# Half of the output weights' combinations move from the expert stage to the gate/value stage, and packed rows are loaded and turned later

## The chip, the cores and the metric

The kernel runs on one core of a Trainium2 chip. The metric is the time of one execution on the device in microseconds (us), median of three runs. TensorE is called PE here, VectorE DVE, ScalarE ACT, GpSimd POOL and SyncE SP. All engines run their own instruction streams and wait for each other through semaphores. DMAs are issued by SP (loads from the inputs) and by POOL (what is stored to and loaded back from DRAM buffers of the kernel, and the indirect ones).

## The reference

Three parts follow one another, all in float32.

```python
def _attn_ref(q, k, v):                      # 4 batches, 12 heads, 448 rows, 64 columns
    scores = scale * np.matmul(q, k.transpose(0, 1, 3, 2)) - np.log(S)
    attn = 1.0 / (1.0 + np.exp(-scores))
    return np.matmul(attn, v)
...
x = np.ascontiguousarray(attn_out.transpose(0, 2, 1, 3)).reshape(B * S, H * D)   # 1792 x 768
...
for e in range(E):                           # _moe_ref: 8 experts, each token to its best one
    mask = expert_idx == e
    h = np.maximum(x[mask] @ w1[e], 0.0)     # 768 -> 1024
    out[mask] = gate_w[mask, None] * (h @ w2[e])
...
gate = 1.0 / (1.0 + np.exp(-(x @ w_gate)))   # _moe2_ref: 768 -> 1536
val = x @ w_val
return (gate * val @ w_out)                  # 1536 -> 768
```

## The kernel before

**Stages.** Attention runs over 24 head pairs and writes rows to a DRAM buffer `xd`. Routing chooses an expert per token. The expert stage takes 14 token tiles of 128 rows, numbered p, and scatters its results to the DRAM buffer `yd`. The gate/value stage and the output stage then run twice, for two halves of 896 rows (`sb` 0 and 1). Their products are done in the way of Strassen, with seven products for eight, so they need sums and differences of weight blocks and of rows ahead of the products. Every float32 operand is split into a high part (ACT copies it, L271 for the expert weights) and a low part (DVE subtracts, L272), and each product is three matmuls.

**Order in the expert stage.** Loop p runs: four `h_chunk(p, c)` (first weights, L1086), the front of p+1 (gather, transposes), four `y_chunk(p-1, c)` (second weights, L1070 to L1072), `y_out(p-1)`, `turn(p)`. `y_out` scales on ACT (L1132) and scatters the tile into `yd` by an indirect DMA of POOL (L1138). After each chunk `split_next` splits the weight chunk that is four ahead into a ring. `turn` transposes h and makes its two parts (`hh` on ACT, `hl` on DVE at L1111). A few small tiles go another way, with `yq` (L1203) as their scatter; their rows are gathered early, and transposed on PE at p = 3 (`xTq`, L1163). Each program line is put on its engine's stream where the Python code stands, so where a call stands in these loops sets what it waits behind.

**Side work hidden in the loops.**

- *Packed weights.* The last stages' weights come packed in 64 bits (`wffP`). `decode_load` loads 1.5 MB through SP, `decode(k, step)` unpacks in three DVE operations (L234, L237, L240) and stores 768 KB by POOL: gate/value weights to `wd[k]`, output weights to `wob[0]`. Most are decoded in attention, four (`DEC_MOE`) in the expert stage at p = 4 to 7, and five (`DIRECT`) in the gate/value stage from the staging tile `stg` into the room `dec`, from which they are used and also stored for the second half.
- *Combinations of the output weights.* `combine_load(k)` loads one of six parts of `wob[0]` (768 KB, L254) into a room `cb`, `combine(k)` makes four sums on DVE (L259 to L262) and stores to `wob[1]` (L263). All six stand in the expert stage, two per p from `COMBINE` = 8: one in h_chunk, one in y_chunk, after c = 1. The first two loads are issued at the end of p = 7.
- *Packed rows.* `y_load(t)` loads 128 finished rows of `yd` (384 KB, L1283, into one of two slots), `y_turn(t)` transposes them on PE (L1295) and copies to `YB` on ACT (L1299), for t = 0 to 6. `YLOADS` gives which are loaded at the end of which p; they are turned in the next p, after y_chunk c = 1 and c = 3. `y_split` makes parts of the rows (L1340, L1341).

**The last stages.** `gv_group` runs the twelve groups g of the gate/value stage; `hooks(n)` puts side work behind the products of a group at seven places (`at_`). In the last group the rows for the output stage are split (`t_split`, L1560, L1561) and the sums of the first results prepared (`s_prep`, L1598, L1600). p2, p5, p6 and p7 are the last four products of a group; each is followed by DVE adding its result (L1443, L1448, L1449) to `G`.

```python
def decode_load(k, src, dst):
    SP.dma_start(src.bitcast(U32), wffP[k].bitcast(U32))
...
            if c == 1 and 0 <= k6 < NWO:
                combine(k6)
                if k6:
                    combine_load(k6 + 1)
...
        for t in YLOADS.get(p, ()):
            y_load(G, t)
```

Of the kernel before, what the change touches and what calls it, by code (L numbers as in the profile page):

```python
# [17 lines left out]
ALU = mybir.AluOpType  # L18
# [49 lines left out]
DIRECT = [3, 5, 7, 9, 11]  # L68
DECODE_IN = {1: 3, 2: 5, 4: 7, 6: 9, 8: 11}
DEC_ORDER = list(range(KF2, NDEC)) + [k for k in range(KF2) if k not in DIRECT] + DIRECT  # L70
YLOADS = {7: (0, 1), 8: (2, 3), 9: (4, 5), 10: (6,)}
COMBINE = 8


_COLS = {}
# [72 lines left out]
def routed_kernel(ctx: ExitStack, tc: tile.TileContext, kqP, vP, emb, tau, w1P, w2P, wffP, cst, out):  # L148
# [98 lines left out]
    def wo_part(i, k):  # L247
        return wob[i][:, :, k * 384 : (k + 1) * 384]

    def combine_room(k):  # L250
        return buf(f"cb{k % 2}", (SB_XA, k % 2 * CH), CH)

    def combine_load(k):
        G.dma_start(combine_room(k).rearrange("p (a m) -> p a m", m=384), wo_part(0, k))  # L254

    def combine(k):

        x = combine_room(k).rearrange("p (a m) -> p a m", m=384)
        V.tensor_sub(x[:, 3], x[:, 2], x[:, 3])  # L259
        V.tensor_tensor(out=x[:, 0], in0=x[:, 3], in1=x[:, 0], op=ALU.add)  # L260
        V.tensor_sub(x[:, 2], x[:, 2], x[:, 0])
        V.tensor_sub(x[:, 1], x[:, 1], x[:, 0])  # L262
        G.dma_start(wo_part(1, k), x)  # L263


    parts = {}
    done_split = [0]
# [1088 lines left out]

    decoded = buf("dec", (SB_G, FH * SB + 2 * YA), CH)

    def w_raw(sb, g, a, b):
        if sb == 0 and g in DIRECT:  # L1360
            return decoded[:, a * YW : b * YW]
        return w_part(g, a, b)

    def w_his(sb, g, half):
# [64 lines left out]
    def gv_group(sb, g, hooks):  # L1429

        i, val = divmod(g, 2)
        a, b, d = [one_bank[2 * k + g % 2][:, :TH] for k in range(3)]
        s1, u2, u4 = temp(sb, "s"), temp(sb, f"u{val}"), temp(sb, "v")
        sg = [temp(sb, f"g{k}") for k in range(4)]

        def mm(o, w, y, first, last):
            product(o, *w_op(sb, g, w), *yop[y], KH, first, last)

        def out(k, ps, u=None):
            f, th = (i, i, i + FH, i + FH)[k], k % 2  # L1440
            if not val:
                if u is not None:
                    V.tensor_tensor(out=sg[k], in0=ps, in1=u, op=ALU.add)  # L1443
                late.append(lambda: A.activation(sg[k], ps if u is None else sg[k], AF.Sigmoid))
                return
            o = g_tile(f, th)
            if u is not None:
                V.tensor_tensor(out=o, in0=ps, in1=u, op=ALU.add)  # L1448
            V.tensor_tensor(out=o, in0=ps if u is None else o, in1=sg[k], op=ALU.mult)  # L1449

        late = []

        def gates():
            while late:
                late.pop(0)()

        def p7():
            mm(d, S3, "T3", True, False)

        def p6():  # L1460
            mm(a, S2, "T2", False, False)
            A.copy(u2, a)

        def p2():
            mm(b, A12, "B21", True, True)
            out(0, b, s1)

        def p5():
            mm(a, S1, "T1", False, False)
            A.copy(u4, a)  # L1470
            gates()

        last = g + 1 == NG
        for n, f in enumerate((p6, p2, p5, p7) if last else (p2, p7, p6, p5) if (sb, g) == (1, 0) else (p7, p6, p2, p5)):
            f()
            if n < 3:
                hooks(n)
        out(3, d, u4)
        hooks(3)
        gates()  # L1480
        if not last:
            gv_first(sb, g + 1)
        hooks(4)
        mm(a, S4, "B22", False, True)
        out(1, a)
        gates()
        hooks(5)
        mm(d, A22, "T4", False, True)
        out(2, d, u2)
        gates()  # L1490
        hooks(6)
# [4 lines left out]
    def gv_stage(sb):  # L1496
        for g in range(NG):
            dec = DECODE_IN.get(g) if sb == 0 else None

            def hooks(at_):  # L1500
                if g == 0:
                    y = {1: sb and "T1", 3: "B22", 4: "T4"}.get(at_)
                    if y:
                        y_split(sb, y)
                if g == 0 and sb and at_ == 5:
                    save_tile()
                if g + 1 < NG:
                    if at_ == 0:
                        w_hi(sb, g + 1, 0)
                        w_sums(sb, g + 1, 0)  # L1510
                    elif at_ == 1:
                        w_sums(sb, g + 1, 1)
                        w_lo(sb, g + 1, 0)
                    elif at_ == 3:
                        w_hi(sb, g + 1, 1)
                    elif at_ == 4:
                        w_lo(sb, g + 1, 1)
                else:
                    if at_ in (3, 4):
                        t_split(sb, 0, at_ - 3)  # L1520
                    elif at_ == 5:
                        s_prep(sb, 0)
                    elif at_ == 6:
                        s_prep(sb, 1)
                        s_prep(sb, 2)
                if dec is not None and at_ >= 4:
                    decode(dec, at_ - 4)
                    if at_ == 6 and dec != DIRECT[-1]:
                        decode_load(DIRECT[DIRECT.index(dec) + 1], stage(), decoded)

            if g == 0:
                if sb:
                    y_split(sb, "T2")
                gv_first(sb, 0)
            gv_group(sb, g, hooks)
            if g + 3 < NG and not (sb == 0 and g + 3 in DIRECT):
                ff_load(g + 3)
            if g >= NG - 3:
                o_load(g - NG + 3)
        o_load(3)  # L1540
# [146 lines left out]
    def ff_first(c):  # L1687
        if c == 0:
            for part in range(2):
                w_sums(0, 0, part)  # L1690
        elif c == 1:
            w_hi(0, 0, 0)
            w_lo(0, 0, 0)
            ff_load(2)
            decode_load(DIRECT[0], stage(), decoded)
        elif c == 2:
            w_hi(0, 0, 1)
            w_lo(0, 0, 1)
        else:
            y_split(0, "T2")  # L1700
            y_split(0, "B21")
# [69 lines left out]
    for p in range(2, NSTAT):  # L1771
        k = p - 4
        dec = 0 <= k < DEC_MOE
        if 0 <= k + 1 < DEC_MOE:
            room = [buf("dw64", SB_Y, 2 * CH), buf("dw32", (SB_Y, 2 * CH), CH)] if k % 2 == 0 else \
                [dp.tile([P, n * CH], F32, tag=f"w{32 * n}", name=f"w{32 * n}_{k}") for n in (2, 1)]
            decode_load(DEC_ORDER[DEC_ATT + k + 1], *room)
        for c in range(NW1):
            h_chunk(p, c)
            if p == 2 and c == NW1 - 2:  # L1780
                front(3, later)
                gather(5)
            elif p == 2 and c == NW1 - 1:
                later.pop()()
            elif p == 3 and c == 0:
                turn(2)
                small_ids()
                gather_small()
            split_next()
            if c == 1 and p - PZ in (0, 1, 3):  # L1790
                small_step((0, 2, 0, 6)[p - PZ])
            y = {(NSTAT - 2, 0): "T2", (NSTAT - 2, 2): "T4"}.get((p, c))
            if y:
                y_sum(0, y)
            y = {(NSTAT - 1, 1): "T3", (NSTAT - 1, 3): "T1"}.get((p, c))
            if y:
                y_split(0, y)
            if p == PZ - 1 and c == 3:
                load_small(1)
            k6 = 2 * (p - COMBINE)  # L1800
            if c == 1 and 0 <= k6 < NWO:
                combine(k6)
                if k6:
                    combine_load(k6 + 1)
            if dec and c % 2 == 0:
                decode(DEC_ORDER[DEC_ATT + k], c // 2)
        if 3 < p < NSTAT - 2:
# [3 lines left out]
        if p > 2:  # L1811
            for c in range(NW2):
                y_chunk(p - 1, c)
                if c == 1 and p - 1 in YLOADS:
                    y_turn(YLOADS[p - 1][0])
                if c == 3 and YLOADS.get(p - 1, ())[1:]:
                    y_turn(YLOADS[p - 1][1])
                split_next()
                if p == NSTAT - 3 and c > 1:
                    y_sum(0, ("T3", "T1")[c - 2])  # L1820
                if p == NSTAT - 2 and c == 2:
                    y_split(0, "B11")
                if c == 1 and 0 <= k6 < NWO:
                    combine(k6 + 1)
                elif c == 3 and 0 <= k6 < NWO - 2:
                    combine_load(k6 + 2)
                if p == PZ - 1 and c == 3:
                    load_small(2)
                if p == NSTAT - 1 and c == 1:
# [22 lines left out]
            gate_e()  # L1852
        if p in (4, 5, 6):
            (lambda: packed_a(Y2[:, 0]), packed_b, packed_c)[p - 4]()
        for t in YLOADS.get(p, ()):
            y_load(G, t)
        if p == PZ + 3:
            begin_ff()
        if p == PZ - 2:
            dp = Region(nc, SB_RT, SB_XP)  # L1860
            load_small(0)
            combine_load(0)
            combine_load(1)

    for c in range(NW2):
        y_chunk(NSTAT - 1, c)
# [53 lines left out]
```

## Time and profile before

| | us |
|---|---|
| median of 3 runs | 982.88 (982.69 to 983.84) |
| profiled execution, its own time | 982.17 |
| span of its instructions | 980.4 |
| PE busy | 936.9 |
| DVE busy | 737.8 |
| ACT busy | 544.6 |
| POOL busy | 146.7 |

The span runs from the first to the last instruction of the profiled execution; the remaining 1.8 us lie around it. Times in the rows further down count from the start of the span. Busy PE time contains waits inside matmuls and stretches at a lower granted clock, so the idle time is not all that can be lost.

### The profile page before, as it was taken

What the parts mean: (1) busy time and instruction counts of PE and PEld (TensorE: products, weight loads), DVE (VectorE), ACT (ScalarE), POOL (GpSimd) and SP (SyncE); (2) the same over time, 40 slices, a digit from 0 to 9 for tenths busy, and PEclk for the clock granted to TensorE, in tenths of its full rate; (3) what the DMA queues carried; (4) which work ended last, traced back from release to release, by engine and by line L of the source; (5) the groups of instructions that cost most, each with busy time, mean ns of one, the idle gap of its engine ahead of it and who ended that gap; (6) DMA issues with size and microseconds to landing.
All of it is one profiled execution on the core that took longest, in us unless ns stands there. A gap on an engine that the chain in (4) does not pass through costs nothing.

```text
span 980.4 us, 14867 instructions
## 1 busy us (share of the span) xinstructions
PE 936.9 (96%) x5757; PEld 787.2 (80%) x5757; DVE 737.8 (75%) x912; ACT 544.6 (56%) x645; POOL 146.7 (15%) x124
## 2 busy tenths in 40 slices
PE   9999999996999979899999999999998999999998
PEld 4555556876888767788888899989997999999998
DVE  6877768887798848778978788857897666658774
ACT  6576776474676645667953234446665433335551
POOL 0011014223052222410610000001120000000011
PEclk9999999997999989999999999999999999999999
DMA  8999876456599989885322543237041111125112
GB/s 307 324 348 332 301 233 233 162 163 227 194 407 414 321 307 383 297 300 167 116 113 88 170 129 129 81 116 286 18 161 49 65 65 65 65 97 194 49 49 81
DMA packets 36974, 186.40 MB, mean 190 GB/s; under 512 B 4680, under 2 KB 6744, under 8 KB 32800
## 3 DMA queue, kind: packets, MB, share of 16 engines
q1 hardware_dynamic: 25680, 134.29, 38.8%
q0 software_dynamic: 11216, 51.09, 14.0%
q8 instruction: 46, 0.75, 0.3%
q14 instruction: 32, 0.26, 0.1%
HBM read 180.94 MB, written 35.88 MB: 221 GB/s over the span
## 4 chain that ended last, share of the span: by engine, by line
PE 61%; DMA 7%; DVE 4%; ACT 2%; issue 2%; POOL 0%; DVEq 0%; ACTq 0%; POOLq 0%
PE pb L1404 14%; PE pb L1403 14%; PE pb L1402 14%; PE h L1086 6%; PE y L1070 3%; PE y L1072 3%; DMA yd<-yo,ridx 2%; PE y L1071 2%; DMA cb<-wob 2%; PE qh L1175 1%; PE qy L1198 1%; DMA wd<-dec 1%; DMA Y<-yd 1%; DMA Y<-xd,idx 1%; DVE rg L272 1%
## 5 line engine op out<-in xcount | busy, mean ns | idle before, releaser
L272 DVE TENSOR_TENSOR rg<-raw,rg 128x1536 fp32r<-128x1536 f32 x104 | 180.2, 1756 | 33.5 <-ACT rg L271 33.4
L271 ACT CAST rg<-raw 128x1536 fp32r<-128x1536 f32 x102 | 150.2, 1480 | 73.3 <-PE y L1071 38.6
L1403 PE MATMUL pb<-yl,wh 128*128 128x448 f32 x288 | 105.9, 368 | 2.2 <-DVE yl L1341 2.2
L1086 PE MATMUL h<-rg,xh 128*128 128x512 f32 x336 | 104.3, 406 | 0.4 <-ACT rg L271 0.3
L1404 PE MATMUL pb<-th,sr 128*128 128x384 f32 x294 | 98.5, 335 | 2.8 <-DVE sr L1600 2.8
L1402 PE MATMUL pb<-th,sr 128*128 128x384 f32 x294 | 98.9, 336 | 0.0
L1403 PE MATMUL pb<-tl,sr 128*128 128x384 f32 x294 | 98.4, 335 | 0.2 <-DVE tl L1561 0.2
L427 ACT ACTIVATE attn<-sc,bias_s 128x896 f32<-128x896 f32 x84 | 79.2, 1004 | 28.4 <-PE sc L425 28.0
L1397 DVE TENSOR_TENSOR wl<-wr,wh 128x1536 fp32r<-128x1536 f32 (+1 forms) x43 | 68.0, 1581 | 16.5 <-ACT wh L1392 13.7
L1086 PEld LDWEIGHTS h<-rg,xh 128*128 128x128 f32 x336 | 62.6, 192 | 15.9 <-issue 2.0
L1072 PE MATMUL y<-rg,hh 128*128 128x384 f32 x192 | 67.4, 351 | 7.4 <-DVE rg L272 7.4
L1070 PE MATMUL y<-rg,hh 128*128 128x384 f32 x192 | 69.4, 362 | 3.1 <-DVEq L1229 3.1
L439 PE MATMUL av<-attn,v 128*64 128x448 f32 (+1 forms) x384 | 70.6, 545 | 0.3 <-DVE xT L444 0.3
L1071 PE MATMUL y<-rg,hl 128*128 128x384 f32 x192 | 67.4, 351 | 1.4 <-DVE hl L1111 1.4
L1392 ACT CAST wh<-wr 128x1536 fp32r<-128x1536 f32 (+1 forms) x43 | 57.3, 1333 | 18.5 <-PE pb L1403 14.3
L1086 PE MATMUL h<-rg,xl 128*128 128x512 f32 x168 | 62.4, 399 | 0.9 <-DVE xl L939 0.9
L1403 PEld LDWEIGHTS pb<-yl,wh 128*128 128x128 f32 x288 | 54.3, 189 | 7.2 <-DVE yl L1341 3.0
L1627 POOL DMA_INDIRECT out<-o,idc x12 | 17.5, 1456 | 271.5 <-ACT o L1645 227.7
L1404 PEld LDWEIGHTS pb<-th,sr 128*128 128x128 f32 x294 | 55.2, 188 | 3.4 <-DVE sr L1600 3.4
L1403 PEld LDWEIGHTS pb<-tl,sr 128*128 128x128 f32 x294 | 55.2, 188 | 0.6 <-DVE tl L1561 0.6
L1402 PEld LDWEIGHTS pb<-th,sr 128*128 128x128 f32 x294 | 55.2, 188 | 0.0
L1598 ACT CAST sr<-G 128x768 fp32r<-128x768 f32 x42 | 35.2, 838 | 28.1 <-PE pb L1403 19.0
(483 smaller groups left out, 2110.7 us busy)
## 6 DMA issues: line engine op xcount, KB each, us to landing
raw<-in_w1P SPq DMA_DIRECT2D x52, 768.0 KB
raw<-in_w2P SPq DMA_DIRECT2D x52, 768.0 KB
q<-wob SPq DMA_DIRECT2D x14, 1152.0 KB
wr<-wd SPq DMA_DIRECT2D x19, 768.0 KB
sg<-in_wffP SPq DMA_DIRECT2D x9, 1536.0 KB
kq<-in_kqP SPq DMA_DIRECT2D x24, 448.0 KB
stg<-in_wffP SPq DMA_DIRECT2D x5, 1536.0 KB
Y<-yd POOLq DMA_DIRECT2D x14, 384.0 KB, 6.2
```

The source lines that it names most:

```text
L271: (hi_eng.tensor_copy if hi_eng else A.copy)(hi, raw)
L272: V.tensor_sub(lo, raw, hi)
L427: A.activation(at_, ps[:, :, :S], AF.Sigmoid, bias=bias_s, scale=1.0 / math.sqrt(HD))
L439: T.matmul(av_t[j * HD : (j + 1) * HD, i % 2, :S], v[rows, j * HD : (j + 1) * HD], at_[rows, j, :], start=(u == first_unit(i)), stop=(u == ...
L1070: T.matmul(o, ah[:, ks], bh[:, w], start=(k == 0), stop=False)
L1071: T.matmul(o, al[:, ks], bh[:, w], start=False, stop=False)
L1072: T.matmul(o, ah[:, ks], bl[:, w], start=False, stop=(k == nk - 1))
L1086: T.matmul(ps[:, half, :], x[:, k * P : (k + 1) * P], w[:, s * 512 : (s + 1) * 512], start=(k == 0 and x is xh and w is hi), stop=(k == KD ...
L1397: V.tensor_sub(w_los(g, half), raw, w_his(sb, g, half))
L1402: T.matmul(o, ah[:, k], bh[:, k], start=(first and k == 0), stop=False, skip_group_check=open_)
L1403: T.matmul(o, ah[:, k], bl[:, k], start=False, stop=False, skip_group_check=open_)
L1404: T.matmul(o, al[:, k], bh[:, k], start=False, stop=(k == n - 1), skip_group_check=open_)
```

## The change

1. Combinations k = 0, 1, 2 stay in the expert stage, one per p, after h_chunk c = 3 of p = 9, 10, 11 (before: from p = 8 on, two per p); each load is issued after y_chunk c = 3 of the p before. Combinations 3, 4, 5 go to groups 3, 5, 7 of the first half's gate/value stage, in two steps of two DVE operations each, with the load a group ahead.
2. `y_load(0)` and `y_load(1)` are issued at the end of p = 8 (before: 7). Turns follow `YTURNS`, and each turn issues the load of t+2 right behind it.
3. The first of the four decode loads of the expert stage moves from the start of p = 3 to behind h_chunk c = 2 of p = 3.
4. Packed weight 3, the first of `DIRECT`, is decoded into a room of its own, `spare`, and no longer into `dec`.
5. In the last group of the first half the products run p6, p7, p5, p2 (before: p6, p2, p5, p7), and `t_split` stands behind the first two of the seven places, at 1 and 2 (before: 3 and 4).

```diff
-YLOADS = {7: (0, 1), 8: (2, 3), 9: (4, 5), 10: (6,)}
-COMBINE = 8
+YTURNS = {(9, "y", 1): 0, (9, "y", 3): 1, (10, "h", 1): 2, (10, "y", 1): 3, (10, "y", 3): 4, (11, "h", 1): 5,
+          (11, "y", 1): 6}
+COMBINE = 9
+COMBINE_IN = {3: 3, 5: 4, 7: 5}
...
     def combine_room(k):
+        if k == 4:
+            return spare
+        if k > 2:
+            return buf("cb", (SB_RING, 2 * GW + 3840), CH)
         return buf(f"cb{k % 2}", (SB_XA, k % 2 * CH), CH)
...
-    def combine(k):
+    def combine(k, steps=(0, 1)):
...
+    def decode_room(g):
+        return spare if g == DIRECT[0] else decoded
+
...
-        for n, f in enumerate((p6, p2, p5, p7) if last else (p2, p7, p6, p5) if (sb, g) == (1, 0) else (p7, p6, p2, p5)):
+        for n, f in enumerate(((p6, p2, p5, p7) if sb else (p6, p7, p5, p2)) if last else (p2, p7, p6, p5) if (sb, g) == (1, 0) else (p7, p6, p2, p5)):
...
-                    if at_ in (3, 4):
-                        t_split(sb, 0, at_ - 3)
+                    if at_ - 1 - 2 * sb in (0, 1):
+                        t_split(sb, 0, at_ - 1 - 2 * sb)
...
+                if sb == 0 and at_ == 2 and g + 1 in COMBINE_IN:
+                    combine_load(COMBINE_IN[g + 1])
+                if sb == 0 and at_ in (2, 6) and g in COMBINE_IN:
+                    combine(COMBINE_IN[g], (at_ // 6,))
...
+        def turn_rows(stage, c):
+            t = YTURNS.get((p, stage, c))
+            if t is not None:
+                y_turn(t)
+                if t + 2 < SB // P:
+                    y_load(G, t + 2)
+
+        if 0 < k + 1 < DEC_MOE:
+            decode_next()
...
-            k6 = 2 * (p - COMBINE)
-            if c == 1 and 0 <= k6 < NWO:
+            k6 = p - COMBINE
+            if c == 3 and 0 <= k6 < 3:
                 combine(k6)
-                if k6:
-                    combine_load(k6 + 1)
+            if k + 1 == 0 and c == 2:
+                decode_next()
+            turn_rows("h", c)
...
-                if c == 1 and 0 <= k6 < NWO:
-                    combine(k6 + 1)
-                elif c == 3 and 0 <= k6 < NWO - 2:
-                    combine_load(k6 + 2)
+                if c == 3 and 0 <= k6 + 1 < 3:
+                    combine_load(k6 + 1)
...
-        for t in YLOADS.get(p, ()):
-            y_load(G, t)
+        if p == 8:
+            y_load(G, 0)
+            y_load(G, 1)
...
-            combine_load(0)
-            combine_load(1)
```

**POOL, from the scatter at the end of p = 7 on.** `yd<-yo` is the scatter of a tile's results, `Y<-yd` the load of packed rows, `cb<-wob` the load of a combination, `wob<-cb` its store, `yq` the small tiles' scatter, `xg` the gather of the next tile. Before:

```order
L1138 DMA yd<-yo_4863,ridx 1920x768
L1283 DMA Y_1890<-yd 128x768 x2
L254 DMA cb_4892<-wob_76 128x4x384
L254 DMA cb_4894<-wob_76 128x4x384
L263 DMA wob_77<-cb_4892 512x1x384
L1203 DMA yd<-yq_4983,rowq 7680x192
L923 DMA xg_4990<-xd,idx 128x768
L263 DMA wob_77<-cb_4894 512x1x384
L254 DMA cb_4892<-wob_76 128x4x384
L1138 DMA yd<-yo_5101,ridx 1920x768
L1283 DMA Y_1890<-yd 128x768 x2
```

Now, from the same scatter on:

```order
L1147 DMA yd<-yo_4864,ridx 1920x768
L1212 DMA yd<-yq_4973,rowq 7680x192
L932 DMA xg_4980<-xd,idx 128x768
L260 DMA cb_5067<-wob_76 128x4x384
L1147 DMA yd<-yo_5071,ridx 1920x768
L1292 DMA Y_1891<-yd 128x768 x2
L1212 DMA yd<-yq_5180,rowq 7680x192
L271 DMA wob_77<-cb_5067 512x1x384
L932 DMA xg_5190<-xd,idx 128x768
L1292 DMA Y_1891<-yd 128x768 x2
L260 DMA cb_5299<-wob_76 128x4x384
L1147 DMA yd<-yo_5301,ridx 1920x768
```

Between the first two scatters stood two loads of packed rows, three of combinations and two stores; one load of a combination is left. The first two loads of packed rows now stand behind the second scatter, and the next two behind a `yq` scatter and a gather.

**DVE, the y_chunks of p = 8 and the front of the next tile** (`rg` is a low part of a weight chunk). Before:

```order
L1111 TENSOR_TENSOR hl_4876<-hTp_4866,hh_4875 128x1024
L272 TENSOR_TENSOR rg_87<-raw_82,rg_86 128x1536
L272 TENSOR_TENSOR rg_89<-raw_83,rg_88 128x1536
L259 TENSOR_TENSOR cb_4892<-cb_4892 128x384
L260 TENSOR_TENSOR cb_4892<-cb_4892 128x384
L261 TENSOR_TENSOR cb_4892<-cb_4892 128x384
L262 TENSOR_TENSOR cb_4892<-cb_4892 128x384
L272 TENSOR_TENSOR rg_91<-raw_84,rg_90 128x1536
L272 TENSOR_TENSOR rg_93<-raw_85,rg_92 128x1536
```

Now:

```order
L1120 TENSOR_TENSOR hl_4877<-hTp_4867,hh_4876 128x1024
L281 TENSOR_TENSOR rg_87<-raw_82,rg_86 128x1536
L281 TENSOR_TENSOR rg_89<-raw_83,rg_88 128x1536
L281 TENSOR_TENSOR rg_91<-raw_84,rg_90 128x1536
L281 TENSOR_TENSOR rg_93<-raw_85,rg_92 128x1536
```

The four operations of the first combination are gone from between the low parts.

**DVE, the end of the first half's last gate/value group** (`pb` are results of the products, `tl` the low parts of the rows and `sr` those of the weights' side for the output stage). Before:

```order
L1443 TENSOR_TENSOR t0g_6135<-pb_6116,t0u_6131 128x448
L1448 TENSOR_TENSOR G_6265<-pb_6115,t0s 128x448
L1449 TENSOR_TENSOR G_6265<-G_6265,t0g_6133 128x448
L1448 TENSOR_TENSOR G_6278<-pb_6117,t0v 128x448
L1449 TENSOR_TENSOR G_6278<-G_6278,t0g_6136 128x448
L1561 TENSOR_TENSOR tl_7119<-q_6991,th_7118 128x1152 x2
L1449 TENSOR_TENSOR G_6265<-pb_6113,t0g_6134 128x448
L1600 TENSOR_TENSOR sr_7134<-G_6265,sr_7134 128x768
```

Now:

```order
L1455 TENSOR_TENSOR t0g_6118<-pb_6099,t0u_6114 128x448
L1577 TENSOR_TENSOR tl_7098<-q_6993,th_7097 128x1152 x2
L1460 TENSOR_TENSOR G_6248<-pb_6098,t0s 128x448
L1461 TENSOR_TENSOR G_6248<-G_6248,t0g_6116 128x448
L1460 TENSOR_TENSOR G_6261<-pb_6100,t0v 128x448
L1461 TENSOR_TENSOR G_6261<-G_6261,t0g_6119 128x448
L1461 TENSOR_TENSOR G_6248<-pb_6096,t0g_6117 128x448
L1616 TENSOR_TENSOR sr_7136<-G_6248,sr_7136 128x768
```

The two `tl` operations move ahead of the four that add p2's and p7's results.

## Rows read from the trace of the kernel before

**Rows 1.** Page, part 1: busy us, share, instructions of each engine.

```profile
PE 936.9 (96%) x5757; PEld 787.2 (80%) x5757; DVE 737.8 (75%) x912; ACT 544.6 (56%) x645; POOL 146.7 (15%) x124
```

**Rows 2.** Waits of PE by releaser: us in total, times, longest.

```profile
PE y L1072 <- DVE rg L272: 7.4, 2, 5.9
PE yTp L1295 <- DMA Y<-yd: 6.3, 3, 3.3
...
PE pb L1404 <- DVE sr L1600: 2.8, 2, 1.4
...
PE pb L1402 <- ACT t0u L1462: 1.8, 2, 1.3
PE xTq L1163 <- DMA Y<-xd,idx: 1.8, 1, 1.8
...
PE pb L1404 <- DVE wl L1397: 0.5, 1, 0.5
```

**Rows 3.** Timeline of PE, p = 8: start, us, operation, [idle before <- releaser].

```profile
363.44 0.69 PE L1072 MATMUL y<-rg,hh 128*128 128x384 f32 x1 [5.95 <-DVE rg L272]
...
369.58 0.34 PE L1070 MATMUL y<-rg,hh 128*128 128x384 f32 x1
369.75 0.33 PE L1071 MATMUL y<-rg,hl 128*128 128x384 f32 x1
```

**Rows 4.** Busy time in windows: length, engines, then PEclk, DMA share, GB/s.

```profile
364.00:369.00 5.00, 5.00 (x17) 5.00 (x16) 5.00 (x4) 1.47 (x1) 1.62 (x2) 0.50 1.00 326
448.00:488.00 40.00, 39.07 (x231) 34.37 (x230) 40.00 (x27) 34.64 (x30) 18.94 (x3) 1.00 0.46 147
416.00:424.00 8.00, 7.34 (x41) 5.77 (x42) 5.02 (x6) 3.94 (x4) 0.37 (x1) 0.79 0.97 332
416.00:448.00 32.00, 30.19 (x194) 25.60 (x195) 23.51 (x18) 22.17 (x21) 4.88 (x5) 0.95 0.73 252
```

**Rows 5.** Timeline of DVE, the first combination, p = 8.

```profile
359.51 0.56 DVE L259 TENSOR_TENSOR cb<-cb 128x384 f32<-128x384 f32 x1 [12.21 <-DMA cb<-wob]
```

**Rows 6.** Timeline of POOL, three of its DMAs in the expert stage.

```profile
349.60 1.14 POOL L1283 DMA_DIRECT2D Y<-yd  x2 [8.19 <-DMA yd<-yo,ridx]
...
374.22 1.60 POOL L1138 DMA_INDIRECT yd<-yo,ridx  x1 [1.08 <-ACT yo L1132]
...
477.27 9.53 POOL L1138 DMA_INDIRECT yd<-yo,ridx  x1 [4.52 <-ACT rg L271]
```

**Rows 7.** DMA issues of 340 to 400: KB each, median us to landing.

```profile
cb<-wob POOLq DMA_DIRECT2D x4, 768.0 KB, 8.9
...
Y<-yd POOLq DMA_DIRECT2D x4, 384.0 KB, 7.2
...
yd<-yo,ridx POOLq DMA_INDIRECT x2, 8.9
yd<-yq,rowq POOLq DMA_INDIRECT x2, 6.7
```

**Rows 8.** DMA issues of 476 to 478, and of 531 to 533.

```profile
yd<-yo,ridx POOLq DMA_INDIRECT x1, 14.6
...
wd<-dec POOLq DMA_DIRECT2D x1, 768.0 KB, 10.3
```

**Rows 9.** Timeline of PE: start of p = 9, a turn, third chunk of p = 10.

```profile
371.55 0.70 PE L1086 MATMUL h<-rg,xh 128*128 128x512 f32 x2
...
390.90 0.85 PE L1295 MATMUL yTp<-cs,Y 128*128 128x128 f32 x6 [1.86 <-DMA Y<-yd]
...
404.02 0.74 PE L1086 MATMUL h<-rg,xh 128*128 128x512 f32 x2
```

**Rows 10.** Timeline of DVE, first half's gate/value stage and its end.

```profile
542.04 0.96 DVE L234 TENSOR_SCALAR dec<-stg 128x1536 uint32<-128x1536 uint32 x1 [2.56 <-DMA wd<-dec]
...
581.42 0.62 DVE L1448 TENSOR_TENSOR G<-pb,t0u 128x448 f32<-128x448 f32 x1 [1.15 <-PE pb L1404]
...
653.82 2.62 DVE L1561 TENSOR_TENSOR tl<-q,th 128x1152 fp32r<-128x1152 f32 x2
```

More of the change, by code (lines that the diff above doesn't have):

```diff
@@ L254, in combine_load @@
         G.dma_start(combine_room(k).rearrange("p (a m) -> p a m", m=384), wo_part(0, k))
-    def combine(k):
+    def combine(k, steps=(0, 1)):
         x = combine_room(k).rearrange("p (a m) -> p a m", m=384)
[L259 to L263, printed above, removed]
+        if 0 in steps:
+            V.tensor_sub(x[:, 3], x[:, 2], x[:, 3])
+            V.tensor_tensor(out=x[:, 0], in0=x[:, 3], in1=x[:, 0], op=ALU.add)
+        if 1 in steps:
+            V.tensor_sub(x[:, 2], x[:, 2], x[:, 0])
+            V.tensor_sub(x[:, 1], x[:, 1], x[:, 0])
+            G.dma_start(wo_part(1, k), x)
+    spare = buf("spare", (SB_G, 3584), CH)
     parts = {}
@@ L1357, in routed_kernel @@
     decoded = buf("dec", (SB_G, FH * SB + 2 * YA), CH)
+    def decode_room(g):
+        return spare if g == DIRECT[0] else decoded
     def w_raw(sb, g, a, b):
         if sb == 0 and g in DIRECT:
-            return decoded[:, a * YW : b * YW]
+            return decode_room(g)[:, a * YW : b * YW]
         return w_part(g, a, b)
@@ L1694, in ff_first @@
             ff_load(2)
-            decode_load(DIRECT[0], stage(), decoded)
+            decode_load(DIRECT[0], stage(), decode_room(DIRECT[0]))
         elif c == 2:
@@ L1773, in routed_kernel, with decode_next @@
         dec = 0 <= k < DEC_MOE
-        if 0 <= k + 1 < DEC_MOE:
+        def decode_next():
             room = [buf("dw64", SB_Y, 2 * CH), buf("dw32", (SB_Y, 2 * CH), CH)] if k % 2 == 0 else \
@@ L1813, in routed_kernel @@
                 y_chunk(p - 1, c)
[L1814 to L1817, printed above, removed]
+                turn_rows("y", c)
                 split_next()
```

## The prediction

> **What bounds the kernel now.** I read the page's busy times first. PE is busy for 96% of the span [rows 1], so a change that removes no product can win only PE's idle time, some 43 us, and what PE loses at a lower granted clock. The second view is PE's waits by releaser, because it says which idle time has one cause [rows 2]. Three of its causes are touched here: the low parts of weight chunks (7.4 us, of which one wait has 5.9), the packed rows (6.3 us in three waits) and, in the last stages, the waits for `t0u`, `wl` and `sr`. The third step is to find each wait in the timeline and ask who was late; DVE and POOL are read only there, since their idle time elsewhere costs nothing.
>
> **The first combination (part 1 of the change).** PE stood for 5.95 us at 363.44, waiting for a low part [rows 3]. DVE was late with it because it had stood 12.21 us in front of the first combination, whose load had not landed [rows 5]. That load was itself late: POOL issued it behind the two loads of packed rows, and those had waited 8.19 us for a scatter to land [rows 6]. The new order on DVE has no combination in p = 8, so the low parts have nothing in front of them, and the wait goes. PE also paid behind it. From 364 to 369, right after the idle time, the granted clock was 0.50, the lower of the two levels (1.2 of 2.4 GHz) [rows 4]. The 19 steps from matmul to matmul from 363.44 to 369.58 took 6.14 us, where one step takes 0.17 at the upper level [rows 3], 3.2 us in all. The loss is 2.9 us. Together this gives **8.8 us**. The ends are 8.8 and 0; zero would need another late input of DVE behind this one, which is rival D.
>
> **Packed rows (parts 1 and 2).** The three waits for them have 6.3 us [rows 2]. Behind the longest, 3.3 us, the mean clock over 416 to 424 was 0.79 [rows 4], which is 0.21 x 8 = 1.7 us lost. At stake: 8.0 us. Are the new loads in time? The first turn now stands where before one stood at 390.90 and waited 1.86 [rows 9]. It is due at 389.04, or 17.5 us after the start of p = 9 at 371.55. Its load comes behind the scatter that was issued at 374.22, 2.7 us after that start [rows 6, 9]. This scatter waited for ACT, which had a copy of packed rows ahead of it, and for POOL, which had a store and a load of combinations ahead; all three are gone there, so I take 1.3 (ends 1.3 and 2.7). That leaves 16.2 us. A scatter (8.9) and a load (7.2) need 16.1 [rows 7]: just in time. The third turn stands before the third h_chunk of p = 10, and that is 404.02 - 390.90 = 13.1 us after the first [rows 9], or 29.3 us after the scatter. Its chain is scatter, load, `yq` scatter (it writes what the loads read, so it waits for them) and load: 8.9 + 7.2 + 6.7 + 7.2 = 30.0 us, 0.7 too late. Later turns again have a scatter and a load in front. I charge 1.0 us for all of it and take **7.0 us**. The ends are 8.0 (no turn waits) and 0 (they wait as long as before, rival A); below zero it is rival C. I stay near the upper end because half of the combinations' transfers leave this stage, and the landings that I used were measured while these were still in the way, at a DMA share near 1.0 [rows 4].
>
> Rows 7 have 7.2 us for a load of 384 KB and 8.9 us for one of 768 KB. The Trainium skill, page "DMA: Bandwidth & Descriptors", section "Anatomy of one DMA — SWDGE (gpsimd) path", has about 2.0 us plus the bytes over 436 GB/s for one such DMA, which makes an estimate of 2.9 and 3.8 us. By that no turn would wait and this term would be 8.0. The trace disagrees, with 7.2 where the page's estimate is 2.9, and the measurement decides.
>
> **The moved combinations in the gate/value stage.** Each is four DVE operations of 0.56 us [rows 5], 2.2 us, put in two steps of 1.1 in groups 3, 5 and 7. In such a group DVE waits 1.15 us for PE in one place [rows 10], so it has one step's length to spare there. I cost them at nothing. If that cover is gone, it is 3 x (2.2 - 1.15) = 3.2 us. In the expert stage DVE does three combinations fewer, but from 448 to 488 it is busy for all of 40 us [rows 4]; the last one now stands before that, in a stretch with 32 - 23.5 = 8.5 us idle on DVE [rows 4]. Nothing is charged; rival B is the other way.
>
> **The room of packed weight 3 (part 4).** At 542.04 the decoding of the next weight waited 2.56 us until the store of the one before had read the room [rows 10]; that store took 10.3 us to land [rows 8]. The delay went on through DVE and ACT to two waits of PE: the longest one for `t0u`, 1.3 us, and the one for `wl`, 0.5 [rows 2]. With a room of its own the store blocks nobody: **1.8 us**. The ends are 1.8 and 0 (when the 1.5 MB load of the packed weight, in flight beside that store, lands no earlier). I take 1.8, as the row names the store as the last to come. The other 0.5 us of the waits for `t0u` stays.
>
> **The last group (part 5).** One of PE's two waits for `sr` is 1.4 us [rows 2]; in front of it on DVE stand two operations `tl` of 2.62 us together [rows 10]. They now run earlier, while PE still has products, but in front of the additions that free PSUM for the next products. Ends: +1.4, and -1.3 (one of the pair becomes the new delay). With nothing to choose between them I take 0.
>
> **The first decode load (part 3).** On SP it now comes behind some loads of weights at p = 3. PE waited 1.8 us there for gathered rows [rows 2], and when they land may hang on what the DMA engines carry beside them. Ends: +1.8 (the gather lands earlier) and -1.8 (the load now meets other transfers that PE needs). I take 0. What it feeds is decoded only in p = 4.
>
> **Sum.** 8.8 + 7.0 + 1.8 = 17.6 us. The profiled execution has 982.17, so 964.6; the median of the runs is 0.7 above that execution, which makes **965.3 us**.
>
> **Rivals.**
>
> A, *the turns are as late as before.* The loads are issued later and now the turns follow sooner. The chain of scatter, load, `yq` and load has 0.1 us to spare at its first turn and -0.7 at its third. Two DMAs that land 1.5 to 2 us later each make turns wait as before. For: nearly every landing is serial. Against: less traffic beside them. The 7.0 go: 972.3 us.
>
> B, *DVE becomes the bound late in the expert stage.* From 448 on it has no idle time [rows 4]. If the last combination (2.2 us) and the parts of the rows, which begin later because the last turns do, slide into that stretch, PE waits there: 2.2 + 3.3 (a delay like the longest before) + 1.7 for the clock behind it = 7.2, or 972.5 us. Against: 8.5 us idle ahead of it.
>
> C, *slower: the chain of packed rows breaks.* Indirect DMAs slow down when DVE is full: one took POOL 9.53 us beside 1.60 of an earlier one [rows 6] and landed after 14.6 instead of 8.9 [rows 7, 8], a factor of 1.64. If p = 9 to 11 become such a place for POOL, each of three turns is late by 16.1 x 0.64 = 10.3 us, 30.9 in all, with three stretches at the lower clock of 2.9 each: 965.3 - 1.0 + 30.9 + 8.7 = 1003.9 us. It is slower than before from the point where 3 x 16.1 x (f - 1) + 8.7 reaches 18.6, at f = 1.21, or a scatter that lands in 10.8 us. Against: the turns stand ahead of the full stretch, and DVE loses work there.
>
> The Trainium skill, page "SBUF — State Buffer", section "Who interferes with whom", speaks for C: a VectorE instruction with two inputs in SBUF contends with a GpSimd instruction that reads SBUF, and the low parts on DVE are of that kind. Rows 6 agree with it in direction (9.53 against 1.60), though they don't show which instruction blocked which.
>
> D, *the change doesn't do what it says at p = 8.* Behind the combination DVE may find that the raw weights are late too, as the DMA engines are full there (share 1.00 [rows 4]). Then the first term goes: 974.1 us. Against: while DVE stood 12 us, SP's loads went on, so chunks should be there.
>
> **How the numbers follow.** Forecast 0.62, with a range of its own of 961 to 970: up by 1.0 (turns), 1.4 and 1.8, down by 1.3 (the scatter as late as before), 1.8 and 1.3. A 0.14, B 0.09, D 0.05, C 0.06; A and D together, at 981.1, or as much otherwise, 0.04. The range 961 to 975 holds the forecast's own and A, B and D, and leaves out C, the pair and the tails, under 0.2. A measurement here can tell about 0.2%, 2.0 us, from no change. Faster by more: 0.62 + 0.14 + 0.09 + 0.05 = 0.90. Within: 0.04. Slower: 0.06.
>
> **What would show it.** After the change PE's wait for the low part at p = 8 should be gone, and the clock there 1.00. The waits of turns for packed rows should sum to under 2 us (forecast), 6 (A) or over 10 (C). The decoding in group 2 should not wait for a store. DVE should wait for the combinations' loads nowhere for more than some tenths, and PE should wait for DVE no longer than before in groups 3, 5 and 7 and after 448. The forecast is wrong if scatters land in over 10 us while turns wait for them, or if a new wait of over 2 us stands anywhere from p = 8 to 13.

## The result, and the profile after

| | before | after |
|---|---|---|
| median, us | 982.79 (982.45 to 983.84, 4 runs) | 965.71 (964.35 to 968.20, 4 runs) |
| profiled execution, us | 982.17 | 966.31 |
| its span, us | 980.4 | 964.2 |

The ratio is 0.9827, with a 95% interval of 0.9805 to 0.985: the change makes the kernel faster by 1.7%, or 17.1 us. Forecast were 965.3 us and a range of 961 to 975. The total was right. The parts were not: two large errors cancelled, so that the total came this close by luck.

The page's first part and PE's waits of the kernel after:

```profile
PE 932.3 (97%) x5757; PEld 784.3 (81%) x5757; DVE 737.5 (76%) x912; ACT 544.6 (56%) x645; POOL 146.8 (15%) x124
```

```profile
PE pb L1414 <- ACT yo L1141: 3.1, 1, 3.1
...
PE y L1081 <- DVE rg L281: 1.5, 1, 1.5
PE pb L1416 <- DVE sr L1616: 1.4, 1, 1.4
...
PE xTq L1172 <- DMA Y<-xd,idq: 1.3, 1, 1.3
...
PE pb L1414 <- DVE G L1460: 1.2, 1, 1.2
...
PE pb L1304 <- DMA Y<-yd: 1.1, 1, 1.1
...
PE pb L1414 <- ACT t0u L1474: 0.8, 1, 0.8
```

Against [rows 2], the wait for a low part is down from 7.4 to 1.5 us, and the turns' waits for packed rows are gone (the 1.1 us at L1304 is another turn, in the second half). Three waits are new: for `yo`, for `G`, and that 1.1.

Waits alone don't say where the time went. For that I set the start of the same matmul in both traces side by side:

| place | before | after | earlier by | of it new |
|---|---|---|---|---|
| p = 3, ahead of the small tiles' transposes | 232.28 | 232.22 | 0.1 | |
| p = 3, behind them and the stretch at the lower clock | 249.99 | 246.20 | 3.8 | 3.7 |
| end of p = 8 | 370.75 | 356.85 | 13.9 | 10.1 |
| last turn of the first half | 440.38 | 419.25 | 21.1 | 7.2 |
| first product of the gate/value stage | 495.40 | 477.75 | 17.7 | -3.5 |
| early in that stage | 509.31 | 494.59 | 14.7 | -2.9 |
| group 2, behind the waits for `t0u` and `wl` | 550.51 | 533.31 | 17.2 | 2.5 |
| output stage, first wait for `sr` | 657.90 | 640.59 | 17.3 | 0.1 |
| first packed row of the second half | 664.01 | 647.78 | 16.2 | -1.1 |

Two turns of 0.6 us each (start of the turn to the start of the next matmul) moved out of p = 8 to later, so p = 8 itself gave 10.1 - 1.2 = 8.9 and the turns 7.2 + 1.2 = 8.4. The last row is the difference of the spans, 16.2.

The granted clock of the places concerned, in the view of windows (length, engines, then PEclk, DMA share, GB/s):

```profile
352.00:357.00 5.00, 5.00 (x31) 4.97 (x30) 4.25 (x3) 3.10 (x3) 1.26 (x2) 1.00 0.89 347
397.00:401.00 4.00, 4.00 (x32) 3.20 (x31) 3.93 (x7) 2.96 (x5) 1.65 (x3) 1.00 0.35 113
478.00:483.00 5.00, 5.00 (x14) 4.44 (x15) 3.17 (x5) 1.49 (x2) 1.75 (x1) 0.50 0.19 79
```

The second y_chunks of p = 8 and the turn at 397.6 run at 1.00 now, where 0.50 and 0.79 stood before [rows 4]. The new stretch at 0.50, the level of 1.2 GHz, is at the start of the gate/value stage, right behind the wait for `yo`.

### The profile page after: what moved, and what is told of

The parts are those of the page before. It is cut to its first block, busy times and chain, and to the rows that moved or that the text cites. A ratio compares the mean times of both kernels' runs of the same rounds, so it can differ in the third digit from the quotient of the medians.

```text
span 964.2 us, 14875 instructions
## 1 busy us (share of the span) xinstructions
PE 932.3 (97%) x5757; PEld 784.3 (81%) x5757; DVE 737.5 (76%) x912; ACT 544.6 (56%) x645; POOL 146.8 (15%) x124
## 4 chain that ended last, share of the span: by engine, by line
PE 68%; DVE 3%; ACT 2%; DMA 2%; issue 1%; ACTq 0%; DVEq 0%; POOLq 0%
PE pb L1415 15%; PE pb L1414 15%; PE pb L1416 15%; PE h L1095 9%; PE y L1079 3%; PE y L1081 3%; PE y L1080 3%; PE qh L1184 2%; PE qy L1207 2%; DMA Y<-xd,idq 1%; PE hTp L1114 1%; DMA Y<-yd 1%; DVE rg L281 1%; PE xTp L941 1%; DVE tl L1577 1%
## 5 line engine op out<-in xcount | busy, mean ns | idle before, releaser
L1079 PE MATMUL y<-rg,hh 128*128 128x384 f32 x192 | 67.5, 351 | 3.4 <-DVEq L1238 3.4
L1081 PE MATMUL y<-rg,hh 128*128 128x384 f32 x192 | 65.5, 341 | 1.5 <-DVE rg L281 1.5
```

Of the source, the lines that this page charges most:

```text
L1079: T.matmul(o, ah[:, ks], bh[:, w], start=(k == 0), stop=False)
L1081: T.matmul(o, ah[:, ks], bl[:, w], start=False, stop=(k == nk - 1))
```

## The experiments

Eleven kernels ran in three groups, each group on one chip beside the kernel before. Between executions and chips the same kernel differs by some 2 us and more (beside the first group the kernel before took 979.6 to 988.4 us; the last section shows one source), so verdicts on a part of 1 to 3 us rest on the traces.

**The new wait at the start of the gate/value stage.** The timeline of the kernel after, ACT and PE:

```profile
474.38 1.30 ACT L1349 CAST y0T2hi<-y0T 128x1344 fp32r<-128x1344 f32 x1
...
475.59 1.31 ACT L1349 CAST y0B21hi<-YB 128x1344 fp32r<-128x1344 f32 x1
...
476.80 0.89 ACT L1141 ACTIVATE yo<-y,gate_s 128x768 f32<-128x768 f32 x1
...
477.75 0.74 PE L1414 MATMUL pb<-y0B11hi,wh 128*128 128x448 f32 x1 [3.11 <-ACT yo L1141]
```

Before, the same matmul started without a wait, ahead of ACT's scaling `yo` of the last tile. The built programs say why. The four PSUM slots of the expert stage are handed out in an order that depends on when earlier ones come free, and the change shifted it. Slot of the last tiles' results by name and first bank:

```
before  h13:6  y12:0  hTp13:4  y13:2
after   h13:2  y12:6  hTp13:4  y13:0
```

`y13` is the last tile's result, which `yo` reads; the gate/value stage puts its first product into bank 0. So the first product has to wait for `yo`, and that stands on ACT behind two copies for later products. Two kernels exchange the banks of the first and third product in that group alone, one made from the kernel after and one from the kernel before:

```diff
-        a = one_bank[g % 2][:, :TH]
+        a = one_bank[g % 2 + 2 * ((sb, g) == (0, 0))][:, :TH]
...
-        a, b, d = [one_bank[2 * k + g % 2][:, :TH] for k in range(3)]
+        a, b, d = [one_bank[2 * k + g % 2][:, :TH] for k in ((1, 0, 2) if (sb, g) == (0, 0) else range(3))]
```

> The changed kernel, with two PSUM banks exchanged in the first gate/value group of the first half (its first product in banks 2 and 3, its third in 0 and 1). In the changed kernel the result of the last expert tile lies in banks 0 and 1, so the first product waits for ACT to scale it. Theory (the bank is the cause of the new 3.1 us wait and of the lower clock behind it, 6.4 us in all): 965.7 - 6.4 = 959.3 us, no wait of PE for yo. Rival (PE would wait as long there for ACT's casts, which stand ahead of that scaling): 965.7 us, a wait of about 3 us under another name.

> The kernel before, with the same exchange of PSUM banks. There the last expert tile's result lies in banks 2 and 3, so the exchange puts the first product where it must wait. Theory (bank): PE waits for yo until about 498.6 instead of starting at 495.4, 3.2 us, and some 3 us follow at the lower clock: 982.8 + 6 = 989 us. Rival (the cause is the changed order of work, not the bank): 982.8 us.

Measured: 961.41 us (ratio to before 0.9772, 0.9741 to 0.9802) and 989.15 us (1.0054, 1.0029 to 1.0079). First the kernel with the exchange made from the one after, then PE in the one made from before:

```profile
473.44 0.36 PE L1414 MATMUL pb<-y0B11hi,wh 128*128 128x448 f32 x1
...
475.78 0.89 ACT L1141 ACTIVATE yo<-y,gate_s 128x768 f32<-128x768 f32 x1
```

```profile
498.24 0.47 PE L1402 MATMUL pb<-y0B11hi,wh 128*128 128x448 f32 x1 [3.10 <-ACT yo L1132]
```

The wait goes with the bank in one kernel and comes with the bank in the other, at 3.1 us both times. Against the kernel after, the first gains 5.8 us between the last turn and the end of the stretch at the lower clock; against the kernel before, the second loses 5.2 us there. Over the medians the first gains 4.3 us, not 6.4; in the first half's gate/value stage its profiled execution was slower by some 2 us at the same clock (last section). The theory holds for the wait; the rival falls. The size was put too high. Of the 6.4 us, 0.3 are a longer wait for `hl_last` (0.9 before, 1.2 after), which the exchange doesn't take away, and the stretch at the lower clock doesn't always follow the wait. With part 4 undone (a run further down) PE waits as long, but its clock stays at 1.00:

```profile
476.19 0.47 PE L1414 MATMUL pb<-y0B11hi,wh 128*128 128x448 f32 x1 [3.10 <-ACT yo L1141]
```

```profile
478.00:483.00 5.00, 5.00 (x27) 4.63 (x26) 2.97 (x5) 2.13 (x3) 0.49 (x1) 1.00 0.19 79
```

In the kernel after, the same window had 0.50. By the place of the matmuls the clock behind the wait costs 0.1 us in that run, 1.6 with part 5 undone and 2.7 in the kernel after. What decides between them is open; shown is a bank's price of 3.1 us, and up to some 3 more.

**What made the packed rows and p = 8 late.** One kernel has part 2 alone, the other all but part 2 (their diffs are the hunks on `YTURNS`, `YLOADS` and `turn_rows` in the change, put in or taken out). Both leave the last result in bank 2, so it is part 2 and the rest of the change together that put it into bank 0.

> The kernel before with part 2 of the change alone (packed rows loaded and turned later; all six combinations stay in the expert stage in their old places). Theory (the wait at p = 8 comes from the combination's load standing behind packed-row loads that wait for a scatter on POOL): that wait goes too, 8.8 us, and the turns' 8.0 us partly, since the combinations' transfers are still in the way: 966 to 974 us, 970 as the middle. Rival (the four DVE operations and the traffic of the combinations are the cost at p = 8): the wait there stays, 975 to 983 us.

> The changed kernel with part 2 undone (packed rows loaded and turned in the old places, all else as changed). The last expert tile's result lies in banks 2 and 3 here, so the wait for yo should be gone (6.4 us less than the changed kernel). Theory (the turns waited because they stood too early after the scatter): the 8.0 us of the turns come back, 965.7 - 6.4 + 8.0 = 967.3 us. Rival (the combinations' transfers made the packed rows late, and these are half gone): no more than 2 us come back, 959 to 961 us.

Measured: 974.47 us (0.9914, 0.9886 to 0.9943) and 962.82 us (0.9791, 0.976 to 0.9823). With part 2 alone, first PE's two long waits there, then POOL, then the landing of the two combinations' loads:

```profile
357.35 0.45 PE L1073 MATMUL y<-rg,hh 128*128 128x384 f32 x1 [1.33 <-DVE rg L273]
384.14 1.02 PE L1296 MATMUL yTp<-cs,Y 128*128 128x128 f32 x6 [4.59 <-DMA Y<-yd]
```

```profile
339.54 1.05 POOL L1139 DMA_INDIRECT yd<-yo,ridx  x1 [3.06 <-ACT yo L1133]
340.60 1.57 POOL L255 DMA_DIRECT2D cb<-wob  x2
...
377.45 1.09 POOL L1284 DMA_DIRECT2D Y<-yd  x2 [7.94 <-DMA yd<-yo,ridx]
```

```profile
cb<-wob POOLq DMA_DIRECT2D x2, 768.0 KB, 14.6
```

At p = 8 DVE still does both combinations, but their loads no longer stand behind packed-row loads that wait for the scatter: they go out at 340.60, 1 us after it, instead of 351 [rows 6]. PE's wait falls from 5.95 [rows 3] to 1.33 us, although the loads need a mean of 14.6 us. By the place of the matmuls p = 8 gives 7.4 us here. So it was the place in POOL's queue, not DVE's work, that cost p = 8 most of its 8.9 us. The turns gain next to nothing in this kernel: they wait 6.1 us in sum, one of them 4.59, about the case of rival A.

With all but part 2, PE's waits show:

```profile
PE yTp L1303 <- DMA Y<-yd: 3.0, 2, 1.6
```

These are 3.0 us instead of 6.3 [rows 2]. Beside the kernel after, this one loses 3.4 us from p = 4 to the last turn. Of the 8.4 us at the turns, then, about 5.0 come from the combinations leaving POOL's queue and the DMA engines, and 3.4 from the later places on top; the later places alone gave nearly nothing. Neither theory was right alone: I had expected 8.0 to come back, the rival at most 2.

**The first decode load (part 3), undone:**

```diff
-        if 0 < k + 1 < DEC_MOE:
+        if 0 <= k + 1 < DEC_MOE:
             decode_next()
...
-            if k + 1 == 0 and c == 2:
-                decode_next()
```

> The changed kernel with part 3 undone (the first decode load of the expert stage again at the start of p = 3). Theory (the load, moved away, lets a scatter ahead of the small tiles' gathers land in 3 instead of 7.7 us, so the gathers are issued 4 us earlier): both waits of PE for gathered rows come back, about 3.1 us in all with a stretch at the lower clock behind them, 3.4 us more than the changed kernel: 969 us. Rival (the difference at p = 3 was that of one execution from another): no change, 965.7 us, and a wait of 1.3 us or less.

Measured: 972.08 us (0.9904, 0.9872 to 0.9935), 6.4 us above the first median of the kernel after and 4.7 above its later one. PE's waits for gathered rows are back:

```profile
PE xTq L1172 <- DMA Y<-xd,idq: 1.9, 1, 1.9
...
PE xTq L1172 <- DMA Y<-xd,idx: 1.6, 1, 1.6
```

POOL and the landing of its scatter, in the kernel before and then after:

```profile
224.81 0.98 POOL L1138 DMA_INDIRECT yd<-yo,ridx  x1 [2.78 <-DVE hl L1111]
234.53 0.98 POOL L1153 DMA_INDIRECT Y<-xd,idq  x1 [8.74 <-DVE rg L272]
```

```profile
yd<-yo,ridx POOLq DMA_INDIRECT x1, 7.7
```

```profile
225.40 0.98 POOL L1147 DMA_INDIRECT yd<-yo,ridx  x1 [2.79 <-DMA yd<-yo,ridx]
230.47 1.54 POOL L1162 DMA_INDIRECT Y<-xd,idq  x1 [4.09 <-DMA raw<-in_w2P]
```

```profile
yd<-yo,ridx POOLq DMA_INDIRECT x1, 3.0
```

Beside the 1.5 MB load the scatter lands after 7.7 us, without it after 3.0, and the gather follows about 2 us behind the landing in both (234.53 - 224.81 - 7.7 = 2.0 and 230.47 - 225.40 - 3.0 = 2.1). The releasers in brackets name other engines, but the gather moves with the scatter's landing. With part 3 undone the scatter lands after 6.9 us and the gather is at 233.52, 2.1 us behind it. The theory holds. From 232 to 246 this kernel loses 3.4 us against the kernel after.

**The room of packed weight 3 (part 4), undone** (`decode_room` returns the common room always).

> The changed kernel with part 4 undone (packed weight 3 decoded into the common room again). Theory: DVE waits about 2.5 us for the store of that weight in group 2, and PE 1.3 and 0.5 us behind it: about 1.9 us more than the changed kernel, 967.6 us. Rival (the combination's transfers now in the same place keep DVE waiting or hide it): no difference in PE's waits.

Measured: 967.89 us (0.9852, 0.9831 to 0.9873). DVE in the kernel after, then DVE and PE with part 4 undone:

```profile
524.81 0.96 DVE L236 TENSOR_SCALAR dec<-stg 128x1536 uint32<-128x1536 uint32 x1 [0.24 <-DMA stg<-in_wffP]
```

```profile
522.39 0.96 DVE L236 TENSOR_SCALAR dec<-stg 128x1536 uint32<-128x1536 uint32 x1 [2.39 <-DMA wd<-dec]
```

```profile
527.81 0.48 PE L1414 MATMUL pb<-y0T1hi,wh 128*128 128x448 f32 x1 [1.13 <-ACT t0u L1474]
530.86 0.47 PE L1416 MATMUL pb<-y0B11hi,wl 128*128 128x448 f32 x1 [0.53 <-DVE wl L1409]
```

The store's wait and both of PE's return, 1.8 us by the place of the matmuls behind them. The medians of this kernel and the kernel after are 2.2 us apart, the profiled executions only 0.4, but this one was spared the lower clock behind `yo`. The kernel after also shows what is late next, the load of the packed weight itself, by 0.24 us.

**The last group (part 5), undone, and then with the banks exchanged as well:**

```diff
-        for n, f in enumerate(((p6, p2, p5, p7) if sb else (p6, p7, p5, p2)) if last ...
+        for n, f in enumerate((p6, p2, p5, p7) if last ...
...
-                    if at_ - 1 - 2 * sb in (0, 1):
-                        t_split(sb, 0, at_ - 1 - 2 * sb)
+                    if at_ in (3, 4):
+                        t_split(sb, 0, at_ - 3)
```

> The changed kernel with part 5 undone (order of the last group's products and place of t_split as before). Theory (the 1.4 us gained at the first sr is given back twice, 1.2 us at the last product of the group and 1.1 us at the first packed row of the second half, whose load can't start earlier than PE's last product of the stage): the two waits go and the one for sr of 1.4 us comes back, 0.9 us less than the changed kernel, 964.8 us. Rival (part 5 is a gain): 1.4 us more, 967.1 us.

> The changed kernel with the two PSUM banks exchanged and part 5 undone: the version that should be fastest if both theories hold, 965.7 - 6.4 - 0.9 = 958.4 us, or 0.9 below the kernel with the banks exchanged alone. If part 5 is a gain, it is 1.4 us above that kernel.

Measured: 963.20 us (0.9804, 0.9785 to 0.9824) and 959.76 us (0.9761, 0.9739 to 0.9783). PE at the end of the stage with part 5 undone, then in the kernel after:

```profile
637.13 0.44 PE L1416 MATMUL pb<-th,sr 128*128 128x384 f32 x1 [1.38 <-DVE sr L1616]
```

```profile
638.31 0.47 PE L1414 MATMUL pb<-y0T4hi,wh 128*128 128x448 f32 x1 [1.21 <-DVE G L1460]
...
647.78 0.87 PE L1304 MATMUL pb<-cs,Y 128*128 128x128 f32 x6 [1.14 <-DMA Y<-yd]
```

One wait of 1.38 us stands against two of 2.35. The first of the two is the price that the prediction named (the additions to `G` come late, and the last product waits for the PSUM that they read). The second shows in POOL's rows, before and after:

```profile
656.50 1.09 POOL L1283 DMA_DIRECT2D Y<-yd  x2 [32.40 <-issue]
```

```profile
640.50 1.08 POOL L1292 DMA_DIRECT2D Y<-yd  x2 [33.60 <-PE pb L1416]
```

The load of the second half's packed rows goes out when the stage's last product is done. In the kernel before, PE then stood 1.4 us until 657.90, and the load used that time; after, PE goes on at 640.59 and meets its turn before the load has landed. A gain was handed on to the next wait. By the place of the matmuls, undoing part 5 wins 1.1 us net.

**The fastest version again, and the decode load later still.** The changed kernel, the version with both mendings, and that version with `decode_next` behind c = 3 instead of c = 2, on one chip:

> The changed kernel itself, beside the two that follow on the same chip. Both theories expect the time of its first runs, about 965.7 us.

> The changed kernel with the banks exchanged and part 5 undone, again, beside the changed kernel. Theory: 6.4 us (bank and the clock behind it) and 1.1 us (part 5) below the changed kernel of the same call, 958 to 960 us. Rival (the earlier difference came from the chip): less than 3 us below it.

> The kernel before this one in the list with the first decode load one place later still (behind h_chunk c = 3 of p = 3). Theory (that load slows the small tiles' gathers when it runs beside them): they land about 2 us earlier, PE's wait for gathered rows of up to 1.3 us and the lower clock behind it go, 1 to 3 us less, 956 to 959 us. Rival (DVE then waits for the load when it decodes at p = 4, and the weight chunks behind it are late): 1 to 4 us more.

Measured: 967.37 us (0.9865, 0.9808 to 0.9922), 958.54 us (0.9769, 0.9727 to 0.9811) and 959.51 us (0.9762, 0.9724 to 0.9799). The mended version is 8.8 us below the changed kernel on the same chip; here the two intervals just touch, while those of its first runs and of the changed kernel's first runs (0.9739 to 0.9783 and 0.9805 to 0.985) don't overlap. It has the lowest median of the study, 1.0 us below the version with the later load, which is no more than these runs can tell apart. Between these two profiled executions lie 11.0 us (spans of 966.0 and 955.0). The traces put 5.0 of them at the banks and 1.2 at the last group; the rest is not from the edits (2.3 stand ahead of the banks, most of them from the first 10 us of the kernel, and some 2.5 come from the pace of the second half's gate/value stage). The later load wins nothing: PE's waits show none for gathered rows in either profile, so the place was already free in that execution, and the gain that I expected could not be seen. The first half of the theory does show: with the load issued 2.4 us behind it, the first gather lands after 4.0 us; in the version without the later load, where 0.7 us lie between the two, it took 8.8. Whether PE gains by that, the run doesn't decide; other executions show a wait of up to 1.3 us there.

## Why the prediction was right, and where it was not

- **The first combination, 8.8 us forecast: 8.9.** The mechanism is shown by the kernel with part 2 alone: taking the load out from behind the scatter took the wait from 5.95 to 1.33 us with DVE's work still there. Rival D, that the raw weights would be late next, falls for the changed kernel: the remaining wait for low parts, 1.5 us, is one at 227.9 that was there before (1.45 at 227.0).
- **Packed rows, 7.0 forecast: 8.4.** The charge of 1.0 was not needed in this execution; in the eight other profiled executions with parts 1 and 2, the turns waited 0 to 0.9 us in sum for packed rows. The chain ran as worked out. In the kernel after, POOL's rows, the first turn, and the landings of 359 to 369:

```profile
359.43 1.61 POOL L1147 DMA_INDIRECT yd<-yo,ridx  x1 [6.16 <-ACT yo L1141]
367.46 1.12 POOL L1292 DMA_DIRECT2D Y<-yd  x2 [6.43 <-DMA yd<-yo,ridx]
377.11 1.29 POOL L1212 DMA_INDIRECT yd<-yq,rowq  x1 [8.52 <-ACT YB L1308]
...
380.62 0.57 POOL L1292 DMA_DIRECT2D Y<-yd  x1
...
456.36 9.52 POOL L1147 DMA_INDIRECT yd<-yo,ridx  x1 [4.56 <-DMA yd<-yq,rowq]
```

```profile
374.88 0.81 PE L1304 MATMUL yTp<-cs,Y 128*128 128x128 f32 x6
```

```profile
Y<-yd POOLq DMA_DIRECT2D x2, 384.0 KB, 7.3
yd<-yo,ridx POOLq DMA_INDIRECT x1, 7.7
```

  Scatter and load took 7.7 + 7.3 = 15.0 us on average where 16.1 were reckoned, and the first turn at 374.88 did not wait. It is as close as the sum said: with the banks exchanged, the same turn waited 0.45 us, in another execution. Rival A did not come true here, but did with part 2 alone; the reason given for staying near the upper end, that half of the combinations' transfers leave, was the part that decided.
- **Rivals B and C** did not come. The scatter that takes POOL 9.52 us is still there, at 456.36, far behind the last turn of the half at 419.25, as the prediction held against C. Its premise, that indirect DMAs slow down when DVE is full, is not what the rows show in general. In the kernel before, a scatter in the same stretch in which DVE has no idle time [rows 4] took POOL 1.01 us, and landed after 3.7:

```profile
448.87 1.01 POOL L1138 DMA_INDIRECT yd<-yo,ridx  x1 [9.57 <-ACT yo L1132]
```

  What made others take over 8 us there is open. DVE did not become the bound at the end of the expert stage: the one wait for DVE that grew there is that for `hl_last`, from 0.9 to 1.2 us.
- **The combinations in the gate/value stage, costed at nothing: right.** PE has no new wait for DVE in groups 3, 5 and 7.
- **The room, 1.8 forecast: 1.8** with part 4 undone.
- **The last group, 0 forecast: -1.1.** The trade between +1.4 and -1.3 was seen, and the 1.2 us wait is the latter end. What failed is that the step ended at the gain: I didn't ask what starts at the moment that had moved. The load of the second half's rows starts with PE's last product, so of whatever PE wins behind that point the load takes back as much as it is then late.
- **The decode load, 0 forecast: +3.7.** This step failed. It looked only at how long the gathers take beside the load, and that did get worse: the first lands after 9.2 us in the kernel after, instead of 5.6. But the gathers start behind a scatter, and that had been slowed from 3.0 to 7.7 us by the same load, so that the first gather now goes out 4.1 us earlier (230.47 for 234.53). The prediction didn't look one DMA ahead on POOL's queue.
- **The banks, no term at all: -6.4 at the start of the gate/value stage in the profiled execution, 0.3 of it the wait for `hl_last`.** The prediction counted the turns' work and their waits, but not that each takes a PSUM slot, and that moving them, with the rest of the change, can alter which slot the last tile gets, some 60 us behind the last turn. Its last part did name the sign ("a new wait of over 2 us"), though only up to p = 13, and this one stands behind it.

Summed: forecast 8.8 + 7.0 + 1.8 = 17.6; measured 8.9 + 8.4 + 3.7 + 2.5 - 6.4 - 1.1 + 0.2 = 16.2 between the profiled executions (the 2.5 are the room and 0.7 that I can't assign). The forecast of the total was good because 3.7 + 1.4 + 0.7 more than foreseen stand against 6.4 + 1.1 not foreseen. That is luck: without the stretch at the lower clock behind `yo`, which one run was spared, this execution would have been 2.7 us shorter, and with the last tile in its old slot 5.8 (the median with the banks exchanged is 961.41 us, at the lower end of the range).

The loads of the first turns took 7.3 us. One load of the same size, at 397.30, landed after 3.3 us, while the DMA share from 397 to 401 was 0.35, in the window shown above. The Trainium skill, page "DMA: Bandwidth & Descriptors", section "Anatomy of one DMA — SWDGE (gpsimd) path", whose rule makes an estimate of 2.9 us, thus comes near that one load and not the others.

## What to carry to other kernels

When work with a buffer from a rotating pool is moved, look up which buffer each later user gets, down to the next stage: a slot that changes hands can cost as much (3.1 us, and up to some 3 more at the lower clock) as the later places of the turns win (3.4 us). A transfer that is late is to be followed up its own queue first, since here each of the three gains on POOL came from what stood one DMA ahead of it. And where a wait is removed, look for what was started at its beginning and had been hiding in it.

## What the runs showed that was not expected

PE's pace in a stage differs between executions at the same granted clock. Two windows, one of the first and one of the second half's gate/value stage, in the kernel after as run again, then in the one with the banks exchanged:

```profile
560.00:600.00 40.00, 40.00 (x200) 37.06 (x199) 33.68 (x45) 15.42 (x23) 2.67 (x4) 1.00 0.54 183
760.00:800.00 40.00, 40.00 (x196) 36.32 (x195) 25.97 (x37) 14.13 (x19) 0.00 (x0) 1.00 0.20 67
```

```profile
560.00:600.00 40.00, 40.00 (x195) 36.33 (x195) 33.13 (x43) 15.38 (x23) 2.67 (x4) 1.00 0.46 154
760.00:800.00 40.00, 40.00 (x199) 37.07 (x198) 25.68 (x35) 15.48 (x22) 0.00 (x0) 1.00 0.18 60
```

PE is busy for all of the 40 us in each, at 1.00, and does 199 or 200 matmuls in one half but 195 or 196 in the other; which half is the slow one changes between the two. A step from matmul to matmul is 0.207 instead of 0.202 us in the timeline. Over a half this makes some 2 us, as much as the smaller parts of the change, so medians and traces can differ by as much. Its cause is open; no run here was made for it.
